# Matrix groups of attention, dense block and routing issued in program order: a fused attention and expert kernel

## The chip, the cores and the metric

The kernel runs on one core of a Trainium2 chip. Five engines work side by side: PE (TensorE: matmuls and transposes), DVE (VectorE), ACT (ScalarE), POOL (GpSimd) and SP (SyncE, which issues most DMAs). The metric is the device time of one execution in microseconds (us), as the median of several runs; lower is better. A trace is taken from one profiled execution and has a time of its own.

## The reference

Three layers, one after the other, on 2304 tokens (4 batches of 576) with 512 features (8 heads of 64):

```python
# 1 attention over a sliding window of 64 keys, per batch and head
scores = q @ k.T / sqrt(64); scores[not (0 <= i - j < 64)] = -1e9
x = softmax(scores) @ v                       # [2304, 512]
# 2 dense block with a rational function in the middle
h = x @ w_in                                  # [2304, 2048]
g = (a0 + a1*h + a2*h**2 + a3*h**3) / (1 + |b0|*|h| + |b1|*h**2 + 1e-6)
x = g @ w_out                                 # [2304, 512]
# 3 one of 8 experts per token
logits = x @ w_gate; e = argmax(logits)
gate = softmax(logits)[e]; eom = sigmoid(x @ w_output_gate)[e]
out = gate * eom * (relu(x @ w1[e]) @ w2[e])  # w1 512x1024, w2 1024x512
```

Everything is float32. Each float32 product of layers 2 and 3 is made of three matmuls on parts of the numbers (high times high, high times low, low times high).

## The kernel before, in words

**Attention** is cut into 36 units: 9 blocks of 256 tokens by 4 pairs of heads. A unit is a chain over the engines: four transposes of k and q on PE (tile tq), copies to the tiles KK (ACT, DVE), four score matmuls (sc), mask and row minimum (DVE, L343), four exponentials (ACT, L349), the reciprocal of the sum (DVE), a multiplication (POOL), four transposes of the result ms (pp), their copy back into ms (ACT or DVE), the product with v (xp, eight small matmuls), and the split of xp into a high part (ACT, L387) and a low part (DVE, L388): x0, later xh and xl, the input of the dense block.

**The dense block** is cut into 72 steps: 9 blocks of 256 tokens by 8 pieces of 256 of the 2048 inner features. A step is 24 matmuls h (128x256), the rational function on ACT, DVE and POOL (tiles e, t, qm, r, then the split of g: high part ACT L167, low part POOL L173), and four steps later 12 matmuls y (128x512). The weights w_in and w_out come as float64 words and are converted on the way (DVE ct and cp, ACT wi and wo). Steps 0 to 6 carry one attention unit each, steps 7 to 13 none, and from step 14 half a unit each, until all are done. Twelve half units are written down ahead of step 0.

**Routing** follows a block when its eight y groups are done: y is copied and negated (ysb, on ACT and DVE) and stored to y_dram; PE transposes it (ytp) and makes logits (lt, lg); DVE takes the argmax; PE counts the ranks (rp); POOL scatters token numbers to t_dram (two indirect DMAs at L596 for each block).

**The experts** work in slots of up to 256 tokens of one expert: a list tl is loaded, POOL gathers the rows (xg, L755), PE transposes them (xtp), ACT and DVE split them (xdh L786, xdl L787), and PE makes hp and yp with the expert's weights (wr, split into wx by ACT L167 and by DVE or POOL L173). Slot 0 begins while the last block of the dense part still runs, and the last block's routing runs beside slots 0 and 1.

**What sets the order.** The code is written out unit by unit and step by step; a scheduler that knows of dependences, priorities and planned times then fixes the order of each engine's instructions, once and for all, before the kernel runs. On the chip every engine takes its own list from the top and waits at an instruction whose inputs are not there. The helper in_turn binds the first matmul of a group behind the last matmul of the group bound before it, so that bound groups keep the order in which the code is written; matmuls outside it are placed freely. Before the change the bound groups are xp, ytp, lt, lg and rp. In the written order a step is: h of the step, then its half units of attention (sc and pp in one half, tq and xp in the other), then y of the step four back, then routing.

Of the kernel before, what the change touches and what calls it, by code (L numbers as in the profile page):

```python
# [23 lines left out]
NQ, TA, VU = 2, 2, 2  # L24
# [12 lines left out]
def kernel(  # L37
# [16 lines left out]
    nc = tc.nc  # L54
# [4 lines left out]
    W = 64  # L59
# [8 lines left out]
    BPS = S // W  # L68
# [39 lines left out]
    qbd = [cols["qbd"][:, i * 512:(i + 1) * 512].rearrange("p (b q) -> p b q", b=4) for i in range(NQ)]  # L108
    kT = [cols["kT"][:, i * (W + TB):(i + 1) * (W + TB)] for i in range(NP)]

    ident = cs[:, C_ID:C_ID + 128]
    qc_col = cs[:, C_QC:C_QC + 1]

    def t2(shape, name, dt=F32):
        return s2.tile(shape, dt, tag="s2", name=name)
# [7 lines left out]
    def pt(shape, name):  # L123
        return ps.tile(shape, F32, tag=name, name=name)
# [7 lines left out]
    def charge(e, c):  # L132
        load[e] += c
# [6 lines left out]
    def pick(**cost):  # L140
        e = min(cost, key=lambda x: load[x] + cost[x])
        load[e] += cost[e]
        return e

    def dve(n, fast=False):
        return 0.07 + n / (1920.0 if fast else 960.0)

    def act(n):
        return ACT0 + n / 1200.0
# [4 lines left out]
    def evac(o, i, n, mul=None):  # L154
        if pick(D=dve(n), A=act(n)) == "D":
            if mul is None:
                nc.vector.tensor_copy(out=o, in_=i)
            else:
                nc.vector.tensor_scalar(out=o, in0=i, scalar1=mul, scalar2=None, op0=ALU.mult)
        elif mul is None:  # L160
            nc.scalar.copy(out=o, in_=i)
        else:
            nc.scalar.mul(out=o, in_=i, mul=mul)
# [7 lines left out]
    def arith(o, a, b, op, n):  # L171
        e = pick(D=dve(n), P=pool(n))
        (nc.vector if e == "D" else nc.gpsimd).tensor_tensor(out=o, in0=a, in1=b, op=op)  # L173
# [3 lines left out]
    def mm(o, lhsT, rhs, start, stop):  # L177
        pe[0] = nc.tensor.matmul(o, lhsT, rhs, start=start, stop=stop).ins  # L178

    def transpose(o, i):  # L180
        n = i.shape[0]
        pe[0] = nc.tensor.transpose(o, i, ident[:n, :n]).ins
# [3 lines left out]
    @contextmanager  # L186
    def in_turn():
        if pe[1] is None:
            yield
        else:  # L190
            with tc.issue_after(pe[1]):
                yield
        pe[1] = pe[0]

    def mm3(o, lh, ll, rh, rl, start, stop):
        mm(o, lh, rh, start, False)
        mm(o, lh, rl, False, False)
        mm(o, ll, rh, False, stop)
# [7 lines left out]
    def bc(ap, shp):  # L206
        return ap.unsqueeze(2).to_broadcast(shp)
# [10 lines left out]
    q_t, k_t, v_t = {}, {}, {}  # L218
# [83 lines left out]
    def at_T(n):  # L302
        u, c = divmod(n, NP)
        tq = pt([128, 2, 2, 128], "tq")
        cc = 2 * (c % 2)
        for a, src in ((0, k_t[n // 2]), (1, q_t[n // 2])):
            for r in range(2):
                nc.tensor.transpose(tq[:, a, r, :], src[:, r, cc:cc + 2, :].rearrange("p h d -> p (h d)"), ident)
        if u:
            if pick(D=dve(W, True), A=act(W), P=0.2) == "P":  # L310
                nc.gpsimd.tensor_copy(out=kT[c][:, :W], in_=kT[c][:, TB:])
            else:
                nc.vector.tensor_copy(out=kT[c][:, :W], in_=kT[c][:, TB:])
        evac(kT[c][:, W:], tq[:, 0].rearrange("d r p -> d (r p)"), TB)
        for hh in range(2):
            lo = 64 * hh
            evac(qbd[n % NQ][lo:lo + 64, :, lo:lo + 64],
                 tq[lo:lo + 64, 1].rearrange("d r (b p) -> d (r b) p", b=2), 256, -scale)

    def spans(nk):  # L320
        a = 0
        while a < 4:
            b = a
            while b < 4 and nk[b] == nk[a]:
                b += 1
            yield a, b, nk[a]
            a = b

    def at_QK(n):
        u, c = divmod(n, NP)  # L330
        sc = pt([128, 4, 128], "sc")
        ms = t2([128, 4, 128], "ms")
        mn = sm.tile([128, 4], F32, tag="mn", name="mn")
        sg = sm.tile([128, 4], F32, tag="sg", name="sg")
        nk = []
        kt = kT[c]
        for i in range(4):
            w = W if (4 * u + i) % BPS == 0 else 2 * W
            mm(sc[:, i, :w], qbd[n % NQ][:, i, :], kt[:, i * W + 2 * W - w:(i + 2) * W], True, True)
            nk.append(w)  # L340
        for i in range(4):
            charge("D", dve(128))
            nc.vector.tensor_tensor_reduce(  # L343
                out=ms[:, i, :nk[i]], in0=sc[:, i, :nk[i]], in1=cs[:, C_MASK + 128 - nk[i]:C_MASK + 128],
                scale=1.0, scalar=3.0e38, op0=ALU.add, op1=ALU.min, accum_out=mn[:, i:i + 1],
            )
        for i in range(4):
            charge("A", act(128))
            nc.scalar.activation(out=ms[:, i, :nk[i]], in_=ms[:, i, :nk[i]], func=AF.Exp,  # L349
                                 scale=-1.0, bias=mn[:, i:i + 1], accum_out=sg[:, i:i + 1])  # L350
        charge("D", 0.2)
        nc.vector.tensor_scalar(out=sg, in0=sg, scalar1=1e-9, scalar2=None, op0=ALU.add)
        nc.vector.reciprocal(out=sg, in_=sg)  # L353
        for a, b, w in spans(nk):
            arith(ms[:, a:b, :w], ms[:, a:b, :w], bc(sg[:, a:b], [128, b - a, w]), ALU.mult, (b - a) * w)
        P_t[n] = (ms, nk)

    def at_PT(n):
        ms, nk = P_t.pop(n)
        pp = pt([128, 4, 128], "pp")  # L360
        pT = ms
        for i in range(4):
            nc.tensor.transpose(pp[:nk[i], i, :], ms[:, i, :nk[i]], ident)
        for a, b, w in spans(nk):
            evac(pT[:w, a:b], pp[:w, a:b], (b - a) * 128)
        pT_t[n] = (pT, nk)
# [27 lines left out]
    def rt_mm1(s):  # L394
        j, fp = seq[s]
        h = pt([128, 2, TB], "h")
        w = wi_t[fp]
        xh, xl = x_t[j]
        for a in range(2):
            f0 = a * 128  # L400
            for c in range(KD):
                mm3(h[:, a, :], w[:, 0, c, f0:f0 + 128], w[:, 1, c, f0:f0 + 128], xh[:, c, :], xl[:, c, :],
                    c == 0, c == KD - 1)
        h_t[s] = h.rearrange("p a t -> p (a t)")
        if j == NB - 1:
            del wi_t[fp]
        if fp == NFP - 1:
            del x_t[j]
# [43 lines left out]
    def rt_mm2(s):  # L452
        j, fp = seq[s]
        nf = HF if j < NG else NFP
        if fp % nf == 0:
            y_t[j] = [pt([128, DM], "y") for _ in range(2)]
        g = g_t.pop(s)
        w = wo_t[fp]
        for t in range(2):
            for a in range(2):  # L460
                f = 2 * fp + a
                o = a * TB + t * 128
                mm3(y_t[j][t], g[:, 0, o:o + 128], g[:, 1, o:o + 128], w[:, 0, a, :], w[:, 1, a, :],
                    f % (2 * nf) == 0, f % (2 * nf) == 2 * nf - 1)
        if j == NB - 1:
            del wo_t[fp]
# [455 lines left out]
    for n in range(NUNIT + 2):  # L922
        first, second = [], []
        if n < NUNIT:
            first.append((at_QK, n))
        if n + TA < NUNIT:
            second.append((at_T, n + TA))
        while done < NUNIT and done <= n - 1:
            first.append((at_PT, done))
            second.append((at_PV, done))  # L930
            done += 1
        evs += [first, second]
# [88 lines left out]
    for n in range(TA):  # L1021
        at_T(n)
# [9 lines left out]
    def step(s):  # L1032
# [14 lines left out]
        if s < NS:  # L1047
            rt_mm1(s)
            rt_head(s)
# [8 lines left out]
        if LAG <= s < NS + LAG:  # L1058
            rt_mm2(s - LAG)
# [102 lines left out]
```

## Time and profile before

| what | value |
|---|---|
| median of 3 runs | 808.91 us (808.74 to 809.58) |
| the profiled execution | 810.46 us |
| its span, first to last instruction | 808.5 us |
| PE busy | 766.3 us (95%) |
| DVE, ACT, POOL busy | 539.0, 506.3, 449.9 us |
| mean granted clock of PE | 0.98 of full |

The profiled execution is 1.55 us over the median, and its span leaves 1.96 us outside the first and last instruction. PE is busy in 95% of the span, so the time is that of PE's work plus the stretches in which it waits, plus what a lower granted clock adds to its matmuls. A row of a timeline gives the start, the duration of a run of equal instructions, engine, line, operation, the tile written and those read, the count, and in brackets the idle time just before it and what ended that.

### The profile page before, as it was taken

The page shows a single profiled execution, that of the slowest core. Times are in us where ns is not written, and L with a number is a line of the kernel's source. Part 1 is how long each engine was busy: PE and PEld are TensorE (multiplying, and loading weights), DVE is VectorE, ACT ScalarE, POOL GpSimd, SP SyncE. Part 2 cuts the span into 40 slices and gives each one's busy share as a digit, 9 for nine tenths or more (in the row PEclk, how much of TensorE's full clock was granted, in tenths as well). Part 3 has the DMA queues.
Part 4 walks back from the last instruction along what each step waited for, and adds up shares of the span by engine and source line. Part 5 has one row for each costly group of instructions (what it writes and reads, how often), then busy time and mean ns, then how long its engine had stood idle before and what let it go on. Part 6 is the DMA issues. An engine that isn't in the chain of part 4 may idle for free. (4 is left out here: it accounts for less than half of the span.)

```text
span 808.5 us, 15245 instructions
## 1 busy us (share of the span) xinstructions
PE 766.3 (95%) x5456; PEld 690.8 (85%) x5456; DVE 539.0 (67%) x1289; ACT 506.3 (63%) x1122; POOL 449.9 (56%) x399
## 2 busy tenths in 40 slices
PE   5868999999999999999999999897998999999994
PEld 4758899888899899999999998786997999999993
DVE  5799999876776766666676667465655456654630
ACT  5889786997766686676676665673525555543420
POOL 2596786665555555565654654675523554556430
PEclk9999999999999999999999999998998999999997
DMA  9786351422321211112120000323618777767610
GB/s 227 223 234 180 92 183 79 131 77 57 84 67 27 51 54 37 41 53 53 27 67 14 1 27 1 101 84 97 243 50 328 273 234 213 239 228 257 212 55 14
DMA packets 105602, 95.26 MB, mean 118 GB/s; under 512 B 77424, under 2 KB 77808, under 8 KB 105520
## 3 DMA queue, kind: packets, MB, share of 16 engines
q1 hardware_dynamic: 101840, 84.49, 35.1%
q0 software_dynamic: 3680, 9.73, 3.2%
q8 instruction: 45, 0.74, 0.4%
q14 instruction: 37, 0.30, 0.1%
HBM read 83.02 MB, written 11.44 MB: 117 GB/s over the span
## 5 line engine op out<-in xcount | busy, mean ns | idle before, releaser
L178 PE MATMUL y<-wo,g 128*128 128x512 f32 x864 | 220.1, 402 | 4.3 <-POOL g L173 3.3
L178 PE MATMUL h<-xh,wi 128*128 128x256 f32 x1024 | 195.8, 284 | 0.0
L178 PEld LDWEIGHTS y<-wo,g 128*128 128x128 f32 x864 | 158.4, 191 | 35.8 <-POOL g L173 3.5
L178 PEld LDWEIGHTS h<-xh,wi 128*128 128x128 f32 x1024 | 164.4, 192 | 2.7 <-DVE xl L388 0.2
L178 PE MATMUL h<-xl,wi 128*128 128x256 f32 x512 | 145.9, 285 | 0.0
L173 POOL TENSOR_TENSOR wx<-wr,wx 128x1024 fp32r<-128x1024 f32 x31 | 83.6, 2707 | 59.8 <-ACT wx L167 51.2
L173 POOL TENSOR_TENSOR g<-t,g 128x512 fp32r<-128x512 f32 x72 | 93.0, 1294 | 40.1 <-ACT g L167 34.8
L178 PE MATMUL hp<-xdh,wx 128*128 128x256 f32 x576 | 109.9, 290 | 3.8 <-ACT xdh L786 3.7
L173 POOL TENSOR_TENSOR qm<-qm,e 128x512 f32<-128x512 f32 x72 | 93.4, 1297 | 35.7 <-ACT qm L420 32.2
L178 PE MATMUL yp<-wx,hT 128*128 128x512 f32 x432 | 101.9, 392 | 0.0
L178 PEld LDWEIGHTS h<-xl,wi 128*128 128x128 f32 x512 | 98.3, 192 | 2.5
L178 PEld LDWEIGHTS hp<-xdh,wx 128*128 128x128 f32 x576 | 93.9, 198 | 5.3 <-ACT xdh L786 4.2
L415 ACT ACTIVATE e<-h 128x512 f32<-128x512 f32 x72 | 43.0, 597 | 87.3 <-PE h L178 87.1
L178 PEld LDWEIGHTS yp<-wx,hT 128*128 128x128 f32 x432 | 80.0, 188 | 16.4 <-DVE hT L794 0.3
L173 DVE TENSOR_TENSOR wx<-wr,wx 128x1024 fp32r<-128x1024 f32 x45 | 69.1, 1545 | 26.0 <-ACT wx L167 25.7
L167 ACT CAST wx<-wr 128x1024 fp32r<-128x1024 f32 x68 | 69.2, 1046 | 27.1 <-DMA wr<-in_moe_w_dram 21.8
L178 PE MATMUL hp<-xdl,wx 128*128 128x256 f32 x288 | 83.1, 290 | 0.7 <-DVE xdl L787 0.7
L440 DVE SCALAR_TENSOR_TENSOR t<-t,KK,r 128x512 f32<-128x512 f32 x72 | 53.6, 744 | 41.0 <-ACT r L434 40.6
L422 POOL TENSOR_SCALAR qm<-e,KK 128x512 f32<-128x512 f32 x45 | 34.6, 768 | 49.4 <-ACT e L415 49.2
L426 DVE TENSOR_TENSOR t<-t,h 128x512 f32<-128x512 f32 x72 | 49.1, 681 | 17.1 <-ACT t L416 17.0
L173 POOL TENSOR_TENSOR ms<-ms,sg 128x512 f32<-128x512 f32 (+4 forms) x60 | 39.2, 669 | 37.0 <-DVE sg L353 19.7
L433 ACT ACTIVATE r<-qm,KK 128x512 f32<-128x512 f32 x72 | 49.5, 688 | 15.3 <-POOL qm L173 14.7
(169 smaller groups left out, 1399.3 us busy)
## 6 DMA issues: line engine op xcount, KB each, us to landing
wr<-in_moe_w_dram SPq DMA_DIRECT2D x80, 512.0 KB, 4.8
stg<-in_moe_w_in_dram SPq DMA_DIRECT2D x8, 1024.0 KB, 6.7
stg<-in_moe_w_out_dram SPq DMA_DIRECT2D x8, 1024.0 KB, 7.4
v<-in_v_dram SPq DMA_DIRECT2D x58, 128.0 KB, 2.8
q<-in_q_dram SPq DMA_DIRECT2D x32, 128.0 KB, 2.8
k<-in_k_dram SPq DMA_DIRECT2D x32, 128.0 KB, 2.9
y_dram<-ysb SPq DMA_DIRECT2D x12, 256.0 KB, 2.1
yp_dram<-yq SPq DMA_DIRECT2D x6, 256.0 KB, 2.6
```

The lines of the kernel that those rows point to most:

```text
L167: nc.scalar.copy(out=o, in_=i)
L173: (nc.vector if e == "D" else nc.gpsimd).tensor_tensor(out=o, in0=a, in1=b, op=op)
L178: pe[0] = nc.tensor.matmul(o, lhsT, rhs, start=start, stop=stop).ins
L415: nc.scalar.activation(out=e, in_=h, func=AF.Abs)
L422: (nc.vector if ef == "D" else nc.gpsimd).tensor_scalar(out=qm, in0=e, scalar1=co[:, 5:6], scalar2=co[:, 4:5], op0=ALU.mult, op1=ALU.add)
L426: nc.vector.tensor_tensor(out=t1, in0=t1, in1=h, op=ALU.mult)
L433: nc.scalar.activation(out=r0, in_=qm_t[s], func=AF.Ln, bias=qc_col)
L440: nc.vector.scalar_tensor_tensor(out=t1, in0=t1, scalar=co[:, 0:1], in1=r0, op0=ALU.add, op1=ALU.mult)
```

## The change

Five more kinds of groups go through in_turn: tq, sc and pp of attention, h and y of the dense block. With xp, ytp, lt, lg and rp, all matmul groups of the three parts now stand on PE in the order in which the code is written. xtp, hp and yp of the expert slots stay free. The two places that called the transpose operation directly call the helper transpose, which does the same operation and notes it for in_turn. No operation is added or removed. Lines behind the edits move by 1 to 5 (L343 becomes L345, L596 becomes L601, L755 L760, L778 L783).

```diff
@@ -303,9 +303,10 @@
         u, c = divmod(n, NP)
         tq = pt([128, 2, 2, 128], "tq")
         cc = 2 * (c % 2)
-        for a, src in ((0, k_t[n // 2]), (1, q_t[n // 2])):
-            for r in range(2):
-                nc.tensor.transpose(tq[:, a, r, :], src[:, r, cc:cc + 2, :].rearrange("p h d -> p (h d)"), ident)
+        with in_turn():
+            for a, src in ((0, k_t[n // 2]), (1, q_t[n // 2])):
+                for r in range(2):
+                    transpose(tq[:, a, r, :], src[:, r, cc:cc + 2, :].rearrange("p h d -> p (h d)"))
         if u:
             if pick(D=dve(W, True), A=act(W), P=0.2) == "P":
                 nc.gpsimd.tensor_copy(out=kT[c][:, :W], in_=kT[c][:, TB:])
@@ -334,10 +335,11 @@
         sg = sm.tile([128, 4], F32, tag="sg", name="sg")
         nk = []
         kt = kT[c]
-        for i in range(4):
-            w = W if (4 * u + i) % BPS == 0 else 2 * W
-            mm(sc[:, i, :w], qbd[n % NQ][:, i, :], kt[:, i * W + 2 * W - w:(i + 2) * W], True, True)
-            nk.append(w)
+        with in_turn():
+            for i in range(4):
+                w = W if (4 * u + i) % BPS == 0 else 2 * W
+                mm(sc[:, i, :w], qbd[n % NQ][:, i, :], kt[:, i * W + 2 * W - w:(i + 2) * W], True, True)
+                nk.append(w)
         for i in range(4):
             charge("D", dve(128))
             nc.vector.tensor_tensor_reduce(
@@ -359,8 +361,9 @@
         ms, nk = P_t.pop(n)
         pp = pt([128, 4, 128], "pp")
         pT = ms
-        for i in range(4):
-            nc.tensor.transpose(pp[:nk[i], i, :], ms[:, i, :nk[i]], ident)
+        with in_turn():
+            for i in range(4):
+                transpose(pp[:nk[i], i, :], ms[:, i, :nk[i]])
         for a, b, w in spans(nk):
             evac(pT[:w, a:b], pp[:w, a:b], (b - a) * 128)
         pT_t[n] = (pT, nk)
@@ -396,7 +399,8 @@
         h = pt([128, 2, TB], "h")
         w = wi_t[fp]
         xh, xl = x_t[j]
-        for a in range(2):
+        with in_turn():
+          for a in range(2):
             f0 = a * 128
             for c in range(KD):
                 mm3(h[:, a, :], w[:, 0, c, f0:f0 + 128], w[:, 1, c, f0:f0 + 128], xh[:, c, :], xl[:, c, :],
@@ -456,7 +460,8 @@
             y_t[j] = [pt([128, DM], "y") for _ in range(2)]
         g = g_t.pop(s)
         w = wo_t[fp]
-        for t in range(2):
+        with in_turn():
+          for t in range(2):
             for a in range(2):
                 f = 2 * fp + a
                 o = a * TB + t * 128
```

**Place 1: the start, PE.** The rows are PE's list where the first steps and the first units meet, before and then of the change (x_202 is the first block's x).

```order
L178 MATMUL h<-x_202,wi 128x256 x28
L178 MATMUL sc<-KK 128x128 x8
L178 MATMUL h<-x_202,wi 128x256 x10
L363 MATMUL pp<-KK,ms 128x128 x4
L178 MATMUL h<-x_202,wi 128x256 x16
L178 MATMUL xp<-ms,v 64x64 x8
L363 MATMUL pp<-KK,ms 128x128 x4
L308 MATMUL tq<-KK,k 128x128 x4
L178 MATMUL xp<-ms,v 64x64 x8
L178 MATMUL h<-x_202,wi 128x256 x2
```

```order
L178 MATMUL h<-x_202,wi 128x256 x24
L178 MATMUL sc<-KK 128x128 x4
L182 MATMUL pp<-KK,ms 128x128 x4
L182 MATMUL tq<-KK,k 128x128 x2
L182 MATMUL tq<-KK,q 128x128 x2
L178 MATMUL xp<-ms,v 64x64 x8
L178 MATMUL sc<-KK 128x128 x4
L182 MATMUL pp<-KK,ms 128x128 x4
L182 MATMUL tq<-KK,k 128x128 x2
L182 MATMUL tq<-KK,q 128x128 x2
```

Before, h matmuls of several steps stand between the links of the attention units; now the units' groups stand together and the 24 h matmuls of a step in one piece. Up to the first y matmul PE has the same work in both lists (120 h matmuls, 12 units' sc, 11 units' pp, 14 units' tq) but for xp, of which ten units stand ahead of it before and eleven now.

The same stretch on ACT, further on: the rows around the copy of pp of unit 10 (pp_1032), which that first y group now stands behind, before and then of the change (ms_1012 is the unit after it, wo_1082 and ct_1083 are converted weights, KK_78 takes the transposed k and q).

```order
L163 ACTIVATE KK_78<-tq_1040 64x4x64 x2
L349 ACTIVATE ms_1012,sg_1014<-ms_1012,mn_1013 128x128
L349 ACTIVATE ms_1012,sg_1014<-ms_1012,mn_1013 128x64
L349 ACTIVATE ms_1012,sg_1014<-ms_1012,mn_1013 128x128 x2
L387 CAST xh_850<-xp_943 128x256
L161 COPY ms_906<-pp_1032 128x128
L161 COPY ms_906<-pp_1032 64x128
L167 CAST g_896<-t1_679 128x512
L161 COPY ms_906<-pp_1032 128x256
```

```order
L438 ACTIVATE r0_1005<-r0_1005 128x512
L351 ACTIVATE ms_1012,sg_1014<-ms_1012,mn_1013 128x128
L351 ACTIVATE ms_1012,sg_1014<-ms_1012,mn_1013 128x64
L351 ACTIVATE ms_1012,sg_1014<-ms_1012,mn_1013 128x128 x2
L167 CAST wo_1082<-ct_1083 128x512
L167 CAST wo_1082<-ct_1090 128x512
L161 COPY ms_906<-pp_1032 128x128
L161 COPY ms_906<-pp_1032 64x128
L161 COPY ms_906<-pp_1032 128x256
```

Two weight casts and the second half of r0_1005 have moved ahead of the copy.

**Place 2: step 68, PE.** The rows are those around the first transposes ytp of block 7, before and then of the change.

```order
L178 MATMUL h<-xh,wi 128x256
L178 MATMUL y<-wo,g 128x512
L182 MATMUL ytp<-KK,ysb 128x128 x4
L178 MATMUL y<-wo,g 128x512 x11
L178 MATMUL h<-xh,wi 128x256
```

```order
L178 MATMUL h<-xh,wi 128x256
L178 MATMUL y<-wo,g 128x512 x12
L182 MATMUL ytp<-KK,ysb 128x128 x4
L178 MATMUL h<-xh,wi 128x256
L178 MATMUL h<-xl,wi 128x256
```

The transposes have moved from behind the first of the twelve y matmuls to behind the twelfth.

**Place 3: the end of the dense block, POOL.** The rows are POOL's list around the scatter of block 7's tokens (t_dram), before and then of the change (g_6992 and g_7018 are the g of steps 70 and 71, wx_ is expert weights, xg_7158 a gather for slot 1).

```order
L173 TENSOR_TENSOR wx_7013<-wr_6974,wx_7013 128x1024
L173 TENSOR_TENSOR qm_6919<-qm_6919,e_6915 128x512
L596 DMA t_dram_77<-KK_78,rk_7034 18688x2 x2
L173 TENSOR_TENSOR g_6992<-t1_6841,g_6992 128x512
L173 TENSOR_TENSOR g_7018<-t1_6916,g_7018 128x512
L173 TENSOR_TENSOR wx_7078<-wr_7049,wx_7078 128x1024
L755 DMA xg_7158<-y_dram_75,gi_7156 128x512
```

```order
L173 TENSOR_TENSOR wx_7013<-wr_6974,wx_7013 128x1024
L173 TENSOR_TENSOR qm_6919<-qm_6919,e_6915 128x512
L173 TENSOR_TENSOR g_6992<-t1_6841,g_6992 128x512
L173 TENSOR_TENSOR g_7018<-t1_6916,g_7018 128x512
L601 DMA t_dram_77<-KK_78,rk_7034 18688x2
L173 TENSOR_TENSOR wx_7078<-wr_7049,wx_7078 128x1024
L601 DMA t_dram_77<-KK_78,rk_7034 18688x2
L760 DMA xg_7158<-y_dram_75,gi_7156 128x512
```

The two scatters stood ahead of both g and now stand behind them, the second one also behind a piece of expert weights.

## Rows read from the trace of the kernel before

**Rows 1.** The page: busy time, share of the span, instructions of each engine.

```profile
PE 766.3 (95%) x5456; PEld 690.8 (85%) x5456; DVE 539.0 (67%) x1289; ACT 506.3 (63%) x1122; POOL 449.9 (56%) x399
```

**Rows 2.** Windows: stretch, its length, busy (count) per engine, PE's clock, DMA share, GB/s.

```profile
0.00:40.00 40.00, 28.50 (x221) 24.81 (x222) 25.96 (x100) 27.30 (x92) 15.77 (x30) 0.96 0.88 227
40.00:75.00 35.00, 26.45 (x259) 23.59 (x258) 32.37 (x104) 31.95 (x97) 29.81 (x38) 0.95 0.79 203
75.00:140.00 65.00, 65.00 (x436) 58.23 (x435) 63.34 (x120) 50.38 (x106) 46.15 (x43) 1.00 0.40 130
140.00:160.00 20.00, 19.03 (x140) 16.97 (x138) 17.54 (x39) 18.86 (x45) 12.61 (x12) 1.00 0.44 132
160.00:516.00 356.00, 356.00 (x2702) 322.92 (x2701) 244.61 (x681) 245.11 (x596) 201.45 (x196) 1.00 0.17 42
516.00:543.00 27.00, 24.89 (x163) 21.97 (x162) 16.23 (x30) 19.80 (x33) 21.50 (x14) 0.94 0.43 134
543.00:569.00 26.00, 21.83 (x102) 17.83 (x101) 15.13 (x43) 11.13 (x18) 13.23 (x9) 0.87 0.35 107
613.00:626.00 13.00, 9.37 (x49) 8.69 (x49) 7.40 (x8) 7.95 (x10) 4.37 (x3) 0.74 0.80 288
```

**Rows 3.** Timeline of PE from 43 to 78 us.

```profile
43.81 0.69 PE L178 MATMUL xp<-ms,v 128*64 128x64 f32 x16
...
48.54 2.88 PE L178 MATMUL h<-x,wi 128*128 128x256 f32 x22
...
61.45 1.24 PE L178 MATMUL xp<-ms,v 128*64 128x64 f32 x32 [3.77 <-DVE t L442]
62.62 2.08 PE L178 MATMUL sc<-KK 128*128 128x128 f32 x8
...
71.16 1.16 PE L178 MATMUL sc<-KK 128*128 128x128 f32 x8
...
74.90 3.02 PE L178 MATMUL y<-wo,g 128*128 128x512 f32 x12
```

**Rows 4.** Timeline of ACT from 45 to 79 us.

```profile
45.33 0.60 ACT L415 ACTIVATE e<-h 128x512 f32<-128x512 f32 x1
...
58.37 0.62 ACT L167 CAST wo<-ct 128x512 fp32r<-128x512 f32 x1
...
70.71 0.58 ACT L434 ACTIVATE r<-r 128x512 f32<-128x512 f32 x1
...
78.65 0.37 ACT L161 COPY ms<-pp 128x256 f32<-128x256 f32 x1
```

**Rows 5.** Timeline of DVE at 34 us: the low part of x of unit 3.

```profile
34.43 0.42 DVE L388 TENSOR_TENSOR x<-xp,x 128x256 fp32r<-128x256 f32 x1
```

**Rows 6.** Timeline of PE, 519 to 618 us.

```profile
519.33 0.39 PE L178 MATMUL y<-wo,g 128*128 128x512 f32 x1
521.83 0.66 PE L182 MATMUL ytp<-KK,ysb 128*128 128x128 f32 x4 [2.11 <-ACT ysb L497]
522.24 4.24 PE L178 MATMUL y<-wo,g 128*128 128x512 f32 x11
...
558.43 3.78 PE L178 MATMUL y<-wo,g 128*128 128x512 f32 x8 [3.33 <-POOL g L173]
...
578.99 1.03 PE L778 MATMUL xtp<-KK,xg 128*128 128x128 f32 x8
...
617.98 0.74 PE L178 MATMUL hp<-xdh,wx 128*128 128x256 f32 x4 [2.98 <-ACT xdh L786]
```

**Rows 7.** Timeline of POOL, 556 to 568 us.

```profile
556.11 0.97 POOL L596 DMA_INDIRECT t_dram<-KK,rk  x1 [3.81 <-ACT g L167]
557.11 2.50 POOL L173 TENSOR_TENSOR g<-t,g 128x512 fp32r<-128x512 f32 x2
...
567.48 0.96 POOL L755 DMA_INDIRECT xg<-y_dram,gi  x1 [0.30 <-issue]
```

**Rows 8.** DMA issues: queue, kind, count, median us from issue to landing.

```profile
xg<-y_dram,gi POOLq DMA_INDIRECT x19, 6.1
```

## The prediction, made before the changed kernel ran

> **What bounds the kernel now.** I read the page first: PE is busy for 766.3 of 808.5 us [rows 1], so some 42 us are waits, and nothing but PE's waits and its clock can be won, since the change leaves the work as it is. Then the windows [rows 2]: from 75 to 140 and from 160 to 516 us PE is busy all the time at full clock, and no order of its list makes that shorter. What is idle lies in the start (11.5 us up to 40, 8.6 from 40 to 75), a little at 140 to 160 (1.0), at the seam between the dense block and the experts (2.1 at 516 to 543, 4.2 at 543 to 569, 3.6 at 613 to 626), and in the tail, which the change does not reach. Last the timelines of these stretches [rows 3, 6], to see for whom PE waits there. In the start ACT is busy for 31.95 of 35 us and DVE for 32.37 [rows 2]: PE is fed by two nearly full engines, and it matters what they are given to do first.
>
> **The start.** The first y matmul stands behind the same h, sc, pp and tq work in both lists and starts at 74.90 us before [rows 3]. From there on PE was full, so the change's price in the start is by how much later this matmul comes. Before, loose h matmuls fill PE while softmaxes run; now h of step 0 stands behind xp of unit 4, and each later step's h behind the xp of one more unit.
>
> When does h of step 0 start? It needs the low part of x of unit 3, which DVE reached at 34.43 [rows 5]; in the new list DVE has two conversions more ahead of it, which I put at 0.6 us each, as ACT's cast of that size [rows 4], so about 36. It also stands behind xp of unit 4: behind that unit's reciprocal come POOL's product, pp, the copy and xp, which I put at 0.6 to 0.9 us each by the rows of PE and ACT [rows 3, 4]; with the reciprocal at about 35 that is 38.0 at the earliest. One and a half more, an estimate, for scores that are now issued only after xp of unit 2 gives 39.5, my value. It is not later than the 44.5 at which that xp ended before (43.81 + 0.69 [rows 3]), when h matmuls stood among the links. 24 matmuls at 2.88/22 are 3.1 us [rows 3]; h of step 0 ends at about 42.5.
>
> Then ACT. From e of step 0 to the last copy of pp of unit 10 ACT took 45.33 to 79.02, 33.7 us [rows 4]. The new list has nearly the same items there: three more casts at 0.51 (0.62 less 0.1 by which ACT's starts stand closer than the durations), one more r and one g at 0.5 each, one copy of tq with its two scalings fewer (1.07): 35.2 us. If ACT never waits more than it did, the copy is done at 42.5 + 35.2 = 77.7 and the first y, behind eight xp matmuls and hops of about 1.0, starts at 78.7: 3.8 us later. As one more unit's xp lies behind it (0.9 us; 32 took 1.24 and 16 took 0.98 [rows 3]), the lower bound is +2.9.
>
> But ACT will wait more. Per unit, PE must do xp (0.9), h (3.1) and sc (0.6, half of 1.16 [rows 3]) between two groups of pp, in this order, and e, t of the step and the four exponentials come only behind h and sc. Following the four lists with the durations of the trace, the copies of pp of units 6 to 10 end at 51.3, 57.8, 65.0, 71.2 and 82.2: 6.2 to 7.2 us each, and 11 for the last, which on ACT now stands behind two casts that wait for DVE's conversions (the change's second fence of ACT). The first y starts at 85.4, 10.5 late; less 0.9 for the xp: **+9.6**. It is an estimate by hand; +2.9 is its floor, and its ceiling is some +15, if each of the five steps loses a microsecond more on hops.
>
> **The middle.** At 140 to 160 PE stood idle for 1.0 [rows 2], waiting for t and for a minimum of attention. With the start later and the two feeders less behind, I expect these waits to go: **-0.9**, between 0 and -1.0. From step 14 on PE's list reads nearly the same in both.
>
> **The seam.** At step 68 PE waits 2.11 us for ysb with eleven y matmuls behind, and these then took 4.24 us [rows 6] where eleven of the y group's pace (3.02/12 = 0.25 [rows 3]) take 2.8. In the new list twelve y stand ahead of ytp and cover 519.33 to 522.3; ysb is there at 521.83. Both are won: -2.1 and -1.5, -3.6 together.
>
> At 555 PE waits 3.33 us for g [rows 6]: POOL makes g of steps 70 and 71 only from 557.11 on, behind the two scatters, the second of which stood from 552.3 to 556.1 waiting [rows 7]. Now both g come first. That is -3.3, and the clock it cost: eight y took 3.78 instead of 2.0 [rows 6], and the hp behind them about 1.0 more: -6.1. The clock of 543 to 569, 0.87 [rows 2], agrees: 0.13/0.5 of 26 us, 6.8 us, at the lower of the two levels, 1.2 GHz, 3.3 of them idle and half of the rest lost, 1.8.
>
> What is late next? The scatters. They run up to 5 us later, and with them the list of slot 1, its gather (issued at 567.48 [rows 7], 6.1 us to land [rows 8], so there at 573.6) and its transposes at 578.99 [rows 6]. The cover is 5.4 us; PE will be about 9 us earlier at this point relative to its work, so 1 us may show, and another 1 for xdh of slot 0, whose transposes now stand among y matmuls: +2. Sum of the seam: **-7.7**, between -11 and 0.
>
> At 617.98 PE waits 2.98 us for xdh of slot 2, idles 3.6 in all, with a clock of 0.74 [rows 2, 6]. ACT made xdh behind two casts whose weights came late by DMA. That is not touched by the change, but half of those transposes now stand ahead of slot 1's last yp matmuls: **-1.7**, between 0 and -5.
>
> **Sum.** +9.6 - 0.9 - 7.7 - 1.7 = -0.7, against the profiled execution 810.46: 809.8, which is 1.55 over the median; put to the median, 808.91 - 0.7 = **808.2**. Two large terms cancel, and each is known to some 4 us.
>
> **The rivals.** *ACT keeps pace.* The start costs only its floor, +2.9, because the lists I followed by hand hold slack, or DVE's conversions come in time for the two casts. Then 808.2 - 6.7 = 801.5. For it: ACT was busy for 31.95 of 35 us in 40 to 75 [rows 2], so it lost at most 3 to PE's order so far. Against: each unit's chain now has a whole h group in it.
>
> *PE falls to the lower clock in the start*, the case on the other side. Place: steps 0 to 4, about 40 to 85 us, where PE will be busy for some 6 us of every 7 to 11. Price: after 3.77 us idle, eight sc took 2.08 instead of 1.16, after 2.11 eleven y took 4.24 instead of 2.8 [rows 3, 6]. An h group at half the clock takes 3.1 us more, and it stands on the chain. It decides from two such groups on: +5.8 (two groups, less what ACT's own work hides), 814.0. The Trainium skill, "TensorE: Matmul & The Clock Gate", Part 1, calls the half rate the engine's default, which only activity lifts; the rows after the two waits agree with it (0.39 us for a y matmul against 0.25).
>
> *The seam gives nothing back.* The scatters, the list, the gather and the transposes of slot 1 come late by as much as the g came early, and PE idles at its lower clock again. Then 808.2 + 7.7 = 815.9. For it: the second scatter is now also behind a piece of expert weights. Against: 5.4 us of cover.
>
> **How the numbers follow.** 0.43 for the forecast, with a range of its own of 805 to 811.5; 0.25 for ACT keeping pace (801.5); 0.20 for the low clock in the start (814.0); 0.12 for the lost seam (815.9). The range 800 to 815.5 leaves out half of the last case and the outer ends. A measurement of this kernel tells 0.2%, 1.6 us, from no change: faster is below 807.3, slower above 810.5. The forecast's own range puts some 0.17 of its chance below, 0.17 between and 0.09 above; with the rivals: faster 0.42, same 0.18, slower 0.40.
>
> **What would show it.** The first y matmul's start in the new trace, 85 (right), 79 (ACT keeps pace) or 90 (low clock, with a clock under 0.9 in the window of 40 to 85). At step 68 no idle time ahead of ytp. No wait y for POOL's g at the end of the dense block. A wait of xtp or hp for slot 1 over 2 us would show the lost seam. The prediction fails if waits appear from 160 to 516, where I forecast none, or if h of step 0 starts outside 38 to 44.5.

## The result, and the profile after

The changed kernel takes 818.64 us (median of 4 runs, 816.16 to 822.69) beside 809.25 us for the kernel before (4 runs): a ratio of 1.0123, 95% interval 1.0095 to 1.0151. It is slower by 9.4 us; I had forecast 808.2 and a range of 800.0 to 815.5. The four runs differ more than those before, and their mean granted clock differs with them: 816.16 us at 0.978, 817.24 at 0.981, 820.04 at 0.973, 822.69 at 0.972. The profiled one is the last, 4.0 us over the median, with a span of 820.9 us, 12.4 more than before: what is read from its trace below is the loss of a long execution, some 3 us more than the medians have.

The windows of the profile after (stretch, length, busy and count of PE, PEld, DVE, ACT, POOL, then PE's clock, DMA share, GB/s):

```profile
0.00:40.00 40.00, 25.27 (x155) 20.70 (x156) 24.75 (x88) 24.62 (x81) 14.27 (x28) 0.80 0.76 215
40.00:75.00 35.00, 25.29 (x211) 22.45 (x210) 29.44 (x90) 26.02 (x80) 22.68 (x27) 0.83 0.64 162
75.00:100.00 25.00, 21.89 (x167) 19.12 (x166) 21.18 (x52) 18.20 (x52) 16.71 (x21) 0.86 0.51 132
100.00:140.00 40.00, 38.41 (x257) 34.45 (x256) 32.37 (x62) 29.34 (x59) 26.20 (x25) 1.00 0.44 136
140.00:160.00 20.00, 20.00 (x132) 18.24 (x131) 18.76 (x39) 16.62 (x30) 15.97 (x13) 1.00 0.23 79
...
540.00:584.00 44.00, 41.37 (x258) 35.59 (x258) 32.39 (x68) 29.99 (x49) 33.10 (x21) 1.00 0.32 110
```

Against [rows 2] the start is worse in two ways. PE idles longer (until 140 us it idled 11.5 + 8.6 us; now 14.7 + 9.7 + 3.1 + 1.6), and its clock is down to 0.80, 0.83 and 0.86 where it was 0.96 and 0.95. The clock has two levels, 1.2 and 2.4 GHz, so a mean of 0.80 over 40 us is 16 us at the lower one; the three windows hold 35 us of it, those of before 6.7. Up to the first y matmul the two lists hold the same work but for one xp (0.9 us), and PE's busy time and clock there are, after and then before:

```profile
0.00:92.93 92.93, 65.37 (x492) 56.07 (x492) 68.93 (x217) 66.36 (x207) 50.01 (x71) 0.83 0.68 183
0.00:74.90 74.90, 54.84 (x476) 48.30 (x477) 58.23 (x202) 59.15 (x189) 45.47 (x67) 0.95 0.84 216
```

So PE idles 7.5 us more there (27.6 instead of 20.1) and is busy for 10.5 us more, 0.9 of it the xp and the rest the same matmuls at the lower level for longer.

PE's timeline of the start (start, duration, what, and in brackets the idle time before and what ended it):

```profile
43.22 3.13 PE L178 MATMUL h<-x,wi 128*128 128x256 f32 x24 [0.39 <-DVE ct L292]
46.19 1.05 PE L178 MATMUL sc<-KK 128*128 128x128 f32 x8
50.23 0.66 PE L182 MATMUL pp<-KK,ms 128*128 128x128 f32 x4 [2.98 <-POOL ms L173]
...
53.47 1.12 PE L178 MATMUL xp<-ms,v 128*64 128x64 f32 x16 [2.15 <-DVE sg L355]
54.53 2.08 PE L178 MATMUL sc<-KK 128*128 128x128 f32 x8
...
60.41 3.80 PE L178 MATMUL h<-x,wi 128*128 128x256 f32 x24
...
76.43 4.26 PE L178 MATMUL h<-x,wi 128*128 128x256 f32 x24
...
88.83 0.55 PE L182 MATMUL pp<-KK,ms 128*128 128x128 f32 x2 [1.15 <-POOL ms L173]
...
92.93 4.45 PE L178 MATMUL y<-wo,g 128*128 128x512 f32 x12
```

The first y starts at 92.93, 18.0 later than before [rows 3]. After the two waits at 50 and 53 us the scores take 2.08 instead of 1.05, and two of the h groups 3.80 and 4.26 instead of 3.13: matmuls at the lower level, part of the time. By its waits PE stands for POOL's product (the softmax's last step) 7.6 us in all, where before it was 1.5 (each row gives the sum, the count and the longest wait; the second row is that of before):

```profile
PE pp L182 <- POOL ms L173: 7.6, 7, 3.0
PE pp L363 <- POOL ms L173: 1.5, 1, 1.5
```

The longest of these waits, 2.98 us, came while PE ran at its full pace (the scores ahead of it took 1.05). POOL made that product only at 49.15, behind two conversions of weights, which had themselves waited for ACT, and a part of step 0's function:

```profile
45.72 2.52 POOL L173 TENSOR_TENSOR wi<-ct,wi 128x512 fp32r<-128x512 f32 x2 [2.82 <-ACT wi L167]
...
49.15 1.03 POOL L173 TENSOR_TENSOR ms<-ms,sg 128x512 f32<-128x512 f32 x1
```

The seam, again PE's timeline:

```profile
537.19 0.28 PE L178 MATMUL h<-xh,wi 128*128 128x256 f32 x1
...
542.53 1.66 PE L178 MATMUL y<-wo,g 128*128 128x512 f32 x6 [0.91 <-ACT ysb L502]
544.03 0.60 PE L182 MATMUL ytp<-KK,ysb 128*128 128x128 f32 x4
...
576.31 4.72 PE L178 MATMUL y<-wo,g 128*128 128x512 f32 x20
...
627.60 0.63 PE L783 MATMUL xtp<-KK,xg 128*128 128x128 f32 x4 [0.44 <-DMA xg<-y_dram,gi]
...
631.52 0.89 PE L178 MATMUL hp<-xdh,wx 128*128 128x256 f32 x4 [2.41 <-ACT xdh L791]
```

The transposes ytp now follow the twelve y matmuls without a wait; what is left is 0.91 us in which a y matmul in the middle of the group waits for ysb. The last y groups run without a wait for g, 20 of them at full clock, and slot 2's transposes wait for their gather by 0.44; the wait for its xdh is 2.41 instead of 2.98. What [rows 6] showed at 521.83 and 558.43 is gone. POOL's timeline shows the new order, both g ahead of the scatters:

```profile
571.74 2.58 POOL L173 TENSOR_TENSOR g<-t,g 128x512 fp32r<-128x512 f32 x2 [4.22 <-issue]
574.84 1.02 POOL L601 DMA_INDIRECT t_dram<-KK,rk  x1 [0.52 <-DVE mx L618]
```

**One measure for all runs.** In every list the h of step 68 has the same work of PE ahead of it (but for the fill of three runs below), and the first ytp of block 7 behind it. It starts at 537.19 us after the change, and before at

```profile
516.45 0.28 PE L178 MATMUL h<-xh,wi 128*128 128x256 f32 x1
```

So 20.7 us are lost ahead of it, and from it to the end of the span it is 283.7 instead of 292.1 us: the seam and the slots win 8.4. The difference is, but for rounding, the 12.4 us of the spans. For the experiments this start was found by counting 24 h matmuls a step in the trace.

### The profile page after: what moved, and what is told of

Its sections match the earlier page's. It is cut to its first block, busy times and chain, and to the rows that moved or that the text cites. A ratio compares the mean times of both kernels' runs of the same rounds, so it can differ in the third digit from the quotient of the medians.

```text
span 820.9 us, 15255 instructions
## 1 busy us (share of the span) xinstructions
PE 774.1 (94%) x5456; PEld 691.3 (84%) x5456; DVE 550.2 (67%) x1289; ACT 507.7 (62%) x1122; POOL 448.5 (55%) x399
## 5 line engine op out<-in xcount | busy, mean ns | idle before, releaser
L178 PE MATMUL y<-wo,g 128*128 128x512 f32 x864 | 216.8, 400 | 0.9 <-ACT ysb L502 0.9
L178 PE MATMUL hp<-xdh,wx 128*128 128x256 f32 x576 | 107.6, 286 | 4.1 <-ACT xdh L791 3.4
L173 POOL TENSOR_TENSOR wx<-wr,wx 128x1024 fp32r<-128x1024 f32 x31 | 81.0, 2621 | 49.7 <-ACT wx L167 36.3
L178 PEld LDWEIGHTS hp<-xdh,wx 128*128 128x128 f32 x576 | 92.0, 194 | 5.2 <-ACT xdh L791 3.9
L173 DVE TENSOR_TENSOR wx<-wr,wx 128x1024 fp32r<-128x1024 f32 x45 | 71.0, 1590 | 26.8 <-ACT wx L167 26.6
```

## The experiments

All kernels are the changed one with one edit. For nine of them the five new uses of in_turn become turn(kind), which binds or not by a condition on the kind and on the step at[0] (it is -1 ahead of step 0):

```diff
+    @contextmanager
+    def turn(kind):
+        if CONDITION:
+            with in_turn():
+                yield
+        else:
+            yield
```

The table has each run's median, the ratio to the kernel before on the same chip with its interval, and from the profiled execution the first y, the start of h of step 68 (h68) and from there to the span's end (rest).

| run | bound or edited | median us | ratio (95%) | first y | h68 | rest |
|---|---|---|---|---|---|---|
| before | | | 1 | 74.9 | 516.5 | 292.1 |
| the change | all | 818.64 | 1.0123 (1.0095 to 1.0151) | 92.9 | 537.2 | 283.7 |
| e1_start_free | from step 7 | 805.67 | 0.9961 (0.9944 to 0.9978) | 74.8 | 521.0 | 283.8 |
| e2_start_only | up to step 6 | 826.79 | 1.0243 (1.0215 to 1.0271) | 91.5 | 534.8 | 289.9 |
| e3_fill4 | fill ahead of pp | 814.09 | 1.0060 (1.0038 to 1.0081) | 86.4 | 529.0 | 283.4 |
| e4_lag2 | pp, xp one unit later | 816.00 | 1.0095 (1.0074 to 1.0117) | 85.6 | 527.4 | 284.1 |
| e5_from_step14 | from step 14 | 806.04 | 0.9946 (0.9929 to 0.9963) | 76.3 | 523.0 | 282.3 |
| e6_attention_only | tq, sc, pp | 822.41 | 1.0149 (1.0131 to 1.0166) | 81.2 | 533.3 | 289.5 |
| e7_h_and_y_only | h, y | 827.67 | 1.0224 (1.0205 to 1.0243) | 97.8 | 544.6 | 281.5 |
| e8_y_only | y | 807.78 | 0.9972 (0.9957 to 0.9987) | 85.3 | 523.6 | 282.6 |
| e9_pairs | units in pairs | 812.34 | 1.0031 (1.0008 to 1.0055) | 88.6 | 526.6 | 285.0 |
| e10_from_step9 | from step 9 | 803.66 | 0.9932 (0.9910 to 0.9953) | 76.4 | 519.4 | 282.9 |
| e11_from_step40 | from step 40 | 801.97 | 0.9901 (0.9876 to 0.9926) | 75.2 | 516.7 | 282.1 |
| e12_y_from_step9 | y from step 9 | 806.58 | 0.9964 (0.9947 to 0.9980) | 76.3 | 524.7 | 281.7 |
| e13_fill10 | more fill ahead of pp | 822.48 | 1.0175 (1.0146 to 1.0204) | 91.5 | 536.5 | 284.2 |
| e14_fill4_fill6 | fill ahead of xp too | 819.54 | 1.0150 (1.0114 to 1.0186) | 91.9 | 535.7 | 282.1 |

The table's last three columns come from one execution each. The first y compares only lists with the same work ahead of it; in e4, e6, e7, e8 and e9 other groups stand there, and h68 counts.

### Start or seam: e1 and e2

```diff
+        if at[0] >= 7:        # e1_start_free
+        if at[0] < 7:         # e2_start_only
```

> The five new kinds of groups are bound in order only from step 7 on; up to there they are placed freely as before. Theory: the whole loss of the change lies in the start (first y matmul at 92.9 instead of 74.9 us) and the seam gains some 7 us, so the first y comes at about 75, the waits for ysb and g at the seam are gone, and the time is 801 to 803 us, 0.8 to 1% under the kernel before. Rival: the binding costs in the dense block as well, or the seam gained only because everything came 19 us later; then no better than 806.

> The five new kinds are bound in order only up to step 6, and free afterwards. Theory: the start loses 18 to 19 us and the seam keeps its two waits, so 826 to 829 us. Rival: a free order behind the start makes good some of the delay by filling PE's later waits; then 820 or less.

With the start free the first y is back at 74.82, and the rest is 283.8 as with the change:

```profile
74.82 3.03 PE L178 MATMUL y<-wo,g 128*128 128x512 f32 x12
```

The loss lies in the start, the gain at the seam: e2, whose 826.79 us came as forecast, has the one without most of the other, the first y at 91.5 and at the seam the two old waits, 3.3 us for g and 2.3 for ysb:

```profile
PE y L178 <- POOL g L173: 3.3, 1, 3.3
PE ytp L182 <- ACT ysb L512: 2.3, 1, 2.3
```

But e1 reached 805.67, near its rival's 806, and not 801 to 803: the binding costs something in the dense block as well. It has a wait of its own, on PE's timeline where step 8 begins (x of block 1 is not ready, and the y group that stood there before is now bound behind this h), and a clock of 0.93 in its window:

```profile
95.65 0.58 PE L178 MATMUL h<-xh,wi 128*128 128x256 f32 x1 [2.58 <-DVE xl L401]
```

### Where to begin binding: e5, e10, e11

```diff
+        if at[0] >= 14:       # e5_from_step14
+        if at[0] >= 9:        # e10_from_step9
+        if at[0] >= 40:       # e11_from_step40
```

> The five new kinds are bound from step 14 on instead of step 7. Theory: what kept e1_start_free from the seam's full gain is its one new wait, 2.6 us of h for DVE's xl at 95.6 with a clock of 0.93 behind it; with step 8 free again that wait is gone, the seam's gain stays, and the time is 801 to 803 us. Rival: the gain of the seam is itself only the 3 us that e1_start_free showed; then 805 to 806.

> The five new kinds are bound from step 9 on. Theory: h of step 8 is free to let y pass while the x of block 1 is awaited (the wait of 2.6 us in e1_start_free), and the waits around 150 us, which e5_from_step14 still had, are gone as in e1_start_free; so 801 to 803 us. Rival: one of the two waits stays or another comes in the steps 9 to 14; 804 to 806.

> The five new kinds are bound from step 40 on alone, so that the list of PE is that of before up to there. Theory: the seam by itself is worth its two waits and the clock behind them, 5 to 7 us, whatever is done ahead of it: 802 to 804 us. Rival: the seam's gain comes with the earlier steps' order: 807 or more.

e5 missed, and its 806.04 is the rival's time, though the rest, 282.3, shows more than the rival's 3 us at the seam. The wait at step 8 is gone, but another stands just behind the new beginning, and the clock of that window is 0.91; the clock of 40 to 75 was 0.85 as well, though the lists of all engines there are those of before:

```profile
40.00:75.00 35.00, 27.55 (x255) 24.68 (x253) 31.75 (x95) 31.93 (x98) 29.80 (x38) 0.85 0.74 197
...
140.00:160.00 20.00, 18.25 (x119) 15.91 (x118) 19.73 (x48) 18.19 (x45) 13.64 (x11) 0.91 0.41 119
```

e10 (803.66) is a little above what I expected, e11 (801.97) just under 802 to 804. Attention goes on up to step 61, yet with the binding from step 40 on h68 comes 0.2 us behind that of the kernel before, and all of the seam's gain stays, 282.1 to the end. This version beats both kernels, by 1.0% and by some 2%. Its windows answer to the fifth and sixth of [rows 2]:

```profile
516.00:543.00 27.00, 26.92 (x178) 23.58 (x177) 18.02 (x29) 21.64 (x35) 22.01 (x15) 1.00 0.46 157
543.00:569.00 26.00, 24.26 (x163) 21.59 (x161) 18.63 (x48) 10.65 (x20) 12.92 (x9) 1.00 0.30 105
```

### Which groups: e6, e7, e8, e12

```diff
+        if kind in ("tq", "sc", "pp"):        # e6_attention_only
+        if kind in ("h", "y"):                # e7_h_and_y_only
+        if kind == "y":                       # e8_y_only
+        if kind == "y" and at[0] >= 9:        # e12_y_from_step9
```

> Only tq, sc and pp are bound (with xp as before); h and y stay free. Theory (the loss in the start comes from h being bound: PE has nothing to do while a unit's softmax is awaited): h fills the waits again, the clock of 40 to 75 us is 0.93 or more, the first y comes at 74 to 80, and the time is 806 to 812, with the waits for ysb and g at the seam as before. Rival (the units' links standing in line are the loss, with or without h): first y at 86 or later and 818 or more.

> Only h and y are bound (with xp as before); tq, sc and pp stay free. Theory: h in one piece behind a unit's xp cannot fill waits, so most of the loss of the start is here: first y at 83 to 92, the seam's gain there too, and 810 to 817 us. Rival (the links in line are the loss): first y at 75 to 79 and 801 to 804.

> Only y is bound (with xp, ytp, lt, lg, rp as before). Theory: the start keeps its h as filler, so the first y comes at 75 to 80; the seam's waits for ysb and g go, since ytp now stands behind the whole y group: 801 to 806 us. Rival: the seam needs h bound too, and the waits for ysb or g stay: 808 or more.

> Only y is bound, and only from step 9 on. Theory: the seam's two waits go when the twelve y of a step stand in one piece ahead of the transposes of ytp, so y alone brings the gain: no wait of ytp for ysb and none of y for POOL's g, and 801 to 804 us. Rival: h, sc, pp and tq are needed as well: the waits stay and 807 or more.

My theory of e6 fell: with h free the start loses nearly as much (h68 at 533.3), the time is the rival's, and the clock of 40 to 75 is 0.81. Whether h is not enough to fill, or comes too early to be there when it is wanted, is not shown; a y also waits 3.5 us for a conversion of weights:

```profile
40.00:75.00 35.00, 26.16 (x209) 23.57 (x210) 26.87 (x78) 26.02 (x74) 21.86 (x25) 0.81 0.62 163
```

e7 is worse still in the start than the whole change (h68 at 544.6, clock 0.76 and 0.75), so binding either half spoils it; 827.67 lies above the 810 to 817 that I expected. Both show by their rest where the seam's gain comes from: 281.5 with h and y bound, 289.5 with attention bound. Binding y alone is enough for it, 282.6 in e8 and 281.7 in e12, with no wait of ytp for ysb or of y for g left, as both theories had it. Their times missed all the same (807.78 above 801 to 806, 806.58 above 801 to 804), and e8's first y came at 85.3, not at 75 to 80. What they lose is again ahead of step 68 (e12 idles 3.1 us in 140 to 160, behind a late pp):

```profile
156.88 0.63 PE L182 MATMUL pp<-KK,ms 128*128 128x128 f32 x4 [2.43 <-DVE t L456]
```

### Order or closeness: e4 and e9

```diff
-        while done < NUNIT and done <= n - 1:
+        while done < NUNIT and done <= n - 2:         # e4_lag2, with one more pass of its loop
```

```diff
+    for n in range(0, NUNIT + 2, 2):                  # e9_pairs, in place of the loop over single units
+        for f, m in ((at_QK, n), (at_PT, n - 2), (at_T, n + TA), (at_PV, n - 2)):
+            evs.append([(f, x) for x in (m, m + 1) if 0 <= x < NUNIT])
```

> The change, with pp and xp of a unit written two units behind its scores instead of one. Theory (in the start PE stands at pp for the product of the unit before, 7.6 us in all, and at xp for the copy, and this waiting lowers the clock): the waits of pp for POOL fall under 3 us, the clock of 40 to 75 rises over 0.9, the first y comes at 80 to 86, and the time is 806 to 812. Rival (ACT and DVE are full, so PE waits elsewhere instead): the first y stays at 90 or later and the time is 816 to 820.

> All five kinds bound as in the change, but the written order takes attention units in pairs: scores of two, pp of the two before, tq of two, xp of two, so that an h group and another pair's groups stand between a unit's scores and its pp, and an h group between its pp and its xp. Theory (the loss in the start is that the written order leaves one unit's links too close to each other, not that an order is fixed): the waits of pp and xp halve, the clock of 40 to 75 us is 0.92 or more, the first y comes at 76 to 83, and the time is 801 to 809 us. Rival (any fixed order loses the fill): first y at 88 or later, 814 us or more.

In e4 the waits of pp for POOL's product are gone from the start, as the theory wanted. But PE waits elsewhere, most of all at xp for the copy of pp, and the clock of 40 to 75 stays at 0.85:

```profile
PE xp L178 <- ACT ms L161: 5.8, 8, 1.8
```

In e9 the waits of xp for the copy fall to 0.9, as do those of pp for POOL, but h, sc and pp wait instead, for low parts of x (4.5), for xh (3.0) and for a copy of KK (3.4):

```profile
PE h L178 <- DVE x L401: 4.5, 2, 2.4
PE pp L182 <- DVE KK L324: 3.4, 1, 3.4
PE sc L178 <- ACT xh L400: 3.0, 1, 3.0
```

h68 comes at 527.4 and 526.6, ten before the change's and ten behind the kernel before. e4's first y came where the theory had it, its clock did not, and its time is at the edge of the rival's. e9's time lies between the two, but its first y (88.6) is the rival's, and its clock of 40 to 75 is 0.85 where the theory wanted 0.92. A wider gap in the written order takes back half; with the other half go new waits at other links and the same low clock.

### The clock and the waiting: e3, e13, e14

These kernels do extra work without use, the fill: matmuls of the identity into a tile that its own group then overwrites.

```diff
+            if n < 12:                                # e3_fill4; e13_fill10 has range(10)
+                for i in range(4):
+                    mm(pp[:, i % 4, :], ident, ident, True, True)
             for i in range(4):
                 transpose(pp[:nk[i], i, :], ms[:, i, :nk[i]])
```

```diff
+            if n < 12:                                # e14_fill4_fill6, beside e3's edit
+                for i in range(6):
+                    mm(xp[:, (i % 2) * 128:(i % 2 + 1) * 128], ident, ident, True, True)
```

> The change, with four extra 128x128 matmuls of the identity into each pp tile of the first 12 units ahead of its transposes, which overwrite them; added work without use, about 1 us a unit at full clock. Theory (PE's low clock is a good part of the loss in the start): the clock of 40 to 75 us rises from 0.83 to over 0.92, an h group there takes 3.1 us instead of 3.8 to 4.3, and the first y comes no later than 91 us in spite of the added work, with a time of 813 to 818. Rival (the loss is only waiting in line, the low clock harms nothing): the first y comes 3 to 8 us later, 95 or more, and the time is 822 or more.

> As e3_fill4, with ten extra matmuls of the identity ahead of each pp of the first 12 units instead of four: about 2.6 us of work without use per unit at full clock, more than most waits there are long. If the lower clock is a loss of its own beside the waiting, the extra work must now show: the clock from 40 to 100 us stays at 0.95 or more as with four, but the first y comes 3 to 8 us later than the 86.4 of e3_fill4, since PE itself becomes what the chain waits for. If instead the waiting alone counts and the four only moved it, the first y comes at 86 to 88 again.

> As e3_fill4, with six extra matmuls of the identity ahead of each xp of the first 12 units too, where e3_fill4 still waited 8.2 us for the copies: in all about 2.6 us of work without use per unit. If a low clock is left to be won there (10 us of 100 in e3_fill4), the clock from 20 to 75 us rises to 0.97 or more and the first y comes at 84 to 86.5; what is left over 74.9 us is then the waiting in line. If the clock has nothing more to give, the first y comes at 88 to 93, and 816 us or more.

The windows of e3 and its first y, to be read against those after the change:

```profile
0.00:40.00 40.00, 27.11 (x204) 23.50 (x204) 27.24 (x99) 25.33 (x84) 17.18 (x31) 0.91 0.84 230
40.00:75.00 35.00, 29.20 (x280) 27.15 (x277) 28.70 (x88) 28.81 (x87) 23.40 (x28) 0.95 0.72 191
75.00:100.00 25.00, 23.00 (x194) 20.46 (x194) 21.54 (x64) 20.98 (x64) 18.27 (x24) 1.00 0.44 117
```

```profile
82.60 1.06 PE L178 MATMUL pp<-KK 128*128 128x128 f32 x8
...
86.36 3.04 PE L178 MATMUL y<-wo,g 128*128 128x512 f32 x12
```

So with more work on PE the clock rises to 0.91, 0.95 and 1.00 and the first y comes 6.6 us earlier, as the theory had it; in time e3 is at 814.09 beside 818.64. e13 holds the clock at 1.00 from the start on:

```profile
0.00:40.00 40.00, 29.74 (x252) 27.00 (x253) 26.24 (x94) 24.80 (x82) 16.75 (x31) 1.00 0.82 221
...
43.40 3.14 PE L178 MATMUL h<-x,wi 128*128 128x256 f32 x24
```

Its first y is at 91.5, 5.1 behind e3, as forecast: there the extra work is longer than the waits that it fills. e14 came out on the side of its rival (91.9, 819.54), so the fill at xp costs more than it wins.

**Is the clock the cause of the 6.6 us?** These runs do not show it, since the fill changes more than the clock. PE's list is that of the change but for the fill, but the scheduler plans with the added time, and from 12 to 15 us on it puts the lists of ACT, DVE and POOL in another order. The copy of pp of unit 10, which the first y stands behind, is one case: on ACT it follows two weight casts in the change (the first two rows) and none in e3 (the third):

```profile
90.48 1.22 ACT L167 CAST wo<-ct 128x512 fp32r<-128x512 f32 x2
91.60 0.68 ACT L161 COPY ms<-pp 128x128 f32<-128x128 f32 x3
84.31 0.41 ACT L161 COPY ms<-pp 128x128 f32<-128x128 f32 x2
```

e2 says more: up to the first y its list of PE is that of the change, without any fill. The windows from h of step 0 to the first y, for the change, e2, e3 and e13:

```profile
43.22:92.93 49.71, 37.49 (x312) 33.19 (x312) 40.96 (x117) 40.03 (x121) 32.85 (x40) 0.86 0.66 168
43.46:91.49 48.03, 35.00 (x317) 30.82 (x313) 40.05 (x117) 39.55 (x121) 32.09 (x39) 0.95 0.63 158
42.78:86.36 43.58, 38.59 (x364) 35.76 (x361) 36.68 (x112) 36.80 (x113) 30.54 (x37) 0.96 0.58 145
43.40:91.47 48.07, 44.57 (x437) 42.29 (x433) 38.74 (x118) 38.62 (x114) 31.70 (x38) 1.00 0.59 150
```

At a clock of 0.95, nearly that of e3, e2 is only 1.7 us shorter than the change: its matmuls take 2.5 us less, and its waits 0.8 us more. e3 is 4.4 us shorter than e2 at nearly the same clock, and it has the fill to do as well. So the level of the clock alone does not make e3's 6.6 us; what part is the clock's and what part comes of lists that were planned anew is not shown. (e2's lists of ACT, DVE and POOL differ from the change's as well, from some 31 us on, so 1.7 is no clean price of the clock either. No run changes the clock alone.)

## Why the prediction was wrong, step by step

**What bounds the kernel** held: no wait came in 160 to 516 us, and the difference lies in PE's waits and its clock at the start, just behind it and at the seam.

**The start** is the step that failed: "+9.6" for the first y 10.5 us late, less 0.9 for the xp. It came 18.0 late, so the term measured 17.1, 7.5 more. Of that, 3.7 us were lost before h of step 0, which started at 43.22 instead of 39.5 (inside the bounds of 38 to 44.5). Its chain began late: I had put the reciprocal of unit 4 at about 35, and POOL's product, which follows it, started at 39.21:

```profile
39.21 1.04 POOL L173 TENSOR_TENSOR ms<-ms,sg 128x512 f32<-128x512 f32 x1 [1.47 <-DVE sg L355]
```

Why it was late is open. A full clock does not bring that h forward by itself: e13 has it at 43.40 at a clock of 1.00, though with the fill ahead of it. The other 3.8 us lie between it and the first y, 49.7 us where I had 45.9. I had followed the lists at full clock there and put the lower clock apart, as a rival of chance 0.20; the clock was 0.86, and the matmuls were the longer for it. How much of the 3.8 a full clock would have given back stays open: e2, with the same list of PE at 0.95, is 1.7 shorter. The waits stood for POOL's product more than for ACT's copy, which I had named.

**The rivals.** The one on the other side, the lower clock, came nearest by its signs: the first y at 92.9 for its 90, and the clock under 0.9. It gave 814.0; the change came to 818.64. Its price did not come as I had worked it out, from two h groups at half the clock, 3.1 us each: two were slowed, by 0.7 and 1.1 us, and the rest of the 35 us at the lower level (from the windows) fell on the other groups, on waits and on the time ahead of h of step 0. The Trainium skill, "TensorE: Matmul & The Clock Gate", Part 1, has half rate as the default that activity lifts. The trace agrees: 0.83 in the window with the waits, 0.95 and 1.00 in those where e3 and e13 fill them. ACT keeping pace and the lost seam did not come.

**The middle**, -0.9: the waits at 140 to 160 are gone, as forecast (20.00 busy). But from the first y to h of step 68 the change takes 444.3 us instead of 441.6, 2.7 more, where the sum had 1.8 less (this term, and the xp that already lay ahead of the first y): 4.5 short, and the sign was wrong. The first y group itself took 4.45 us instead of 3.02, and 100 to 140 has 1.6 us of new waits, which I had not seen; the rest is not traced. From 160 us on no wait followed.

**The seam and slot 2**, -7.7 and -1.7, together -9.4: measured -8.4 from h of step 68 on, and -10.0 in e11. The ytp stall went but for the 0.91 us of a y matmul, the one for g went altogether, with its clock, and what is late next, the gather of slot 1's rows, showed no wait of PE, where I had set 1 us. e8 and e12 show that the binding of y did this.

**The sum** put a small remainder of two large terms at -0.7. The seam's term was right to about a microsecond; the start's was 7.5 us short and the middle's 4.5, in the trace of a long execution. My range's upper end, 815.5, leaned on a low clock that I had priced as a separate, small event. (By the chances given, "same" should read 0.17 and "slower" 0.41; nothing hangs on it.)

## What to carry to other kernels

An order that is written down is worth what stands next to each wait: a group of twelve y matmuls in one piece covered a late copy and came with a better order of POOL's work, while in the start the same rule put more waits between the links of a softmax. So bind order stretch by stretch and measure each; here binding from step 40 on gives 801.97 us, 1% under the kernel before, and binding everywhere 1.2% over it.

When a change adds many waits of 1 to 3 us to PE, put the lower clock inside the term, together with the waits, and not into a rival: here such a stretch ran at 0.80 to 0.86. But do not take every slow matmul for lost time: e2 had the same list of PE at 0.95 instead of 0.86 from h of step 0 on, and the stretch was 1.7 us shorter. Matmuls without use ahead of the waits did hold the clock up (0.91 to 1.00 with four, 1.00 with ten). They can tell clock and waiting apart only if the lists of the other engines stay as they were, and here those changed.

## What the runs showed of the hardware

Six kernels have the same lists on PE, ACT, DVE and POOL up to the first y (before, e1, e5, e10, e11, e12). The clock granted from 40 to 75 us was 0.95 in the traces of before and e1, 0.90 in that of e11 and 0.85 in those of e5, e10 and e12, and the first y came at 74.9 and 74.8, at 75.2, and at 76.3 to 76.4 us. So the same instructions are granted another clock in another execution, and here 7 us more at the lower level went with 1.4 to 1.6 us of time; that the clock alone made the difference is not shown.

Whole times spread too. The change's four runs span 6.5 us, but that is not special to it: 29 runs of the kernel before on one chip span 806.65 to 815.01 us, the fastest at a mean clock of 0.989 and the slowest at 0.973. A difference of a few microseconds between two single traces can be no more than this.
